# Convolution and gate of two batches on both query parts at once, with five head-pair slots and mask rows copied by engines

## The chip, the cores and the metric

The kernel runs on one core of one Trainium2 chip. A core has a matrix engine (TensorE, PE in the profile; its weight loads are listed as PEld), a vector engine (VectorE, DVE), a scalar engine (ScalarE, ACT), a general engine (GpSimd, POOL) and a queue engine that mostly issues transfers (SyncE, SP). The metric is the device time of one execution in microseconds. A profiled execution also has a span, which is the time from its first to its last instruction and lies a little below its device time.

## The reference, cut to what matters

Two layers follow each other. The first is block-sparse attention with 4 batches, 8 heads, 768 positions and 64 dimensions: blocks of 32 positions are seen if they are neighbours, first, last, or drawn at random. The second is a feed-forward layer with a gate that comes from a convolution along the sequence:

```python
scores = scale * np.matmul(q, k.transpose(0, 1, 3, 2))
scores = np.where(mask, scores, -1000000000.0)
attn = softmax(scores)                      # over the last axis
x = np.matmul(attn, v)                      # -> (4, 768, 512)
h = np.maximum(x @ w_in, 0.0)               # (4, 768, 1024)
hp = h with one zero position on each side
conv_out = sum(conv_w[k] * hp[:, k:k + S, :] for k in range(3))
gate = 1.0 / (1.0 + np.exp(-conv_out))
out = h * gate @ w_out                      # (4, 768, 512)
```

Inputs and output are float32; the matrix products run in bfloat16.

## The kernel before, in words

**Halves and units.** The 768 queries of a batch are cut into two parts of 384, so that there are 8 halves (`n`, with batch `b` and part `g`). The positions lie in tiles such that position p * 3 + c of a part is in column c * 128 + p, so neighbours along the sequence are 128 columns apart. Attention runs in 144 units, 18 to a half. A unit computes the transposed scores of eight 128x128 blocks on PE into `st` (L678), one exponential of 1024 columns on ACT into `pt` (L685), and the products with the values on PE into `av` (L705). The mask is added inside the score product: the operands have 88 rows, 64 of q or k and 24 that hold the mask in factored form.

**Head pairs and slots.** Heads are handled in 16 pairs, `P`. A pair's q and k come by DMA from POOL's queue (`swdge`, L492) as `nat`, and lie transposed in one of six slots: `ET` holds one head's part of each tile, `OT` the other. Pairs below `NPE` = 6 are transposed on PE (`pe_head`, L533) and moved from PSUM by four DVE copies (L539). Later pairs are transposed by two DMAs on SP's queue (L581) into `tmp`, then copied by two DVE copies of 1536 columns (L424). The 24 mask rows of slot 0 are computed at the start; slot 1 takes them by a DVE copy (ET) and a POOL copy (OT, L453), slots 2 to 5 by eight DMAs on SP's queue (L445).

**After attention.** `norm_ops` divides by the row sums on DVE (L629, L631), and the result is transposed to `xT`: by PE for half 0 and the last piece, else by DMAs on SP's queue (L652). `ffn1` multiplies with `w_in` on PE (L729) for each of eight 128-row chunks `ffc`, and a ReLU on ACT (L740) or DVE (L742), whichever the planner finds free, writes 384 columns into the middle of `hE` [128, 8, 640].

**Convolution and gate.** For two chunks at a time (4 times a half, 32 times in all) POOL copies shifted edges into `hE` (L829 to L835), so that each tap of the convolution is a shifted window of it. `conv_gate` then runs on DVE: three taps, each as two products of 384 columns with a per-partition weight (L753), two adds of 768 columns (L759). ACT applies tanh to 768 columns (L769), DVE adds 1 (L772) and multiplies with h into `gT` (L781). The last column of part 0 needs a neighbour in part 1: its partial sum is saved by POOL (`cvl`, L844), and completed after part 1's ReLUs by three small DVE instructions and a small tanh (L859, L860, L864, L867). `out_block` multiplies with `w_out` (L799), copies to `o2s` and stores through SP.

**What sets the order.** No engine order is written by hand. Each operation is given to `Scheduler` with the engines it may run on, a planned duration, its dependencies and the buffers that it takes and uses. `forward` builds the order of every engine: it takes repeatedly the operation that can start earliest, ties going to the higher priority; `backward` derives new priorities from the order found; `run` repeats this `PASSES` times. Buffers come from pools of fixed size (`P_he`, `P_cv`, `P_gt`, `P_slot` and so on) in turn. `FLEX` decides between ACT and DVE for the operations that either can do. Constants such as `OFF`, `F2A`, `XLAT`, `TLAT` and `S_FIRST` set the due times and assumed transfer latencies of the first pass.

Of the kernel before, what the change touches and what calls it, by code (L numbers as in the profile page):

```python
# [48 lines left out]
FLEX = 0.0345  # L49
# [4 lines left out]
class Scheduler:  # L54
# [108 lines left out]
    def backward(self, order):  # L163
# [34 lines left out]
        for o, t in zip(order, end):  # L198
            o.prio = -t
            o.outs = []  # L200
            for b in o.allocs:
                b.index = None
                b.pool.holders = []
# [10 lines left out]
def kernel(  # L214
# [21 lines left out]
    NSLOT = 6  # L236
    NPE = 6
# [21 lines left out]
    NTMP, NVN, NNAT, NPT, NXK, NXT, NHE, NCV, NGT, NOS = 2, 3, 3, 5, 3, 4, 3, 3, 4, 4  # L259
# [7 lines left out]
    hE_t = many(NHE, [128, NFFC, 640], BF16, "hE")  # L267
    m_t = many(NCV, [128, 2, 768], BF16, "m")
    tn_t = many(NCV, [128, 768], BF16, "tn")
    gT_t = many(NGT, [128, NFFC, 384], BF16, "gT")  # L270
# [48 lines left out]
    T0, PACE0, PACE1 = 8.0, 0.91, 1  # L319
    OFF = 32.0894  # L320
    XLAT, TLAT = 3.908, 9.2201
    S_FIRST, A_FIRST, R_FIRST, N_FIRST = 5.6663, -4, 0.1178, 0.842
    F1S, F2A, F2S = 0.03, 2.344, 0.191
    WO = 22.9467
    OFFL = 28
    PE_ = 0.0
    PASSES = 12
# [116 lines left out]
    def rows_to(dst, src):  # L444
        return lambda e: nc.sync.dma_start(out=dst[64:88], in_=src[64:88])  # L445

# [9 lines left out]
    for s in range(1, NSLOT):  # L456
        for t, m in ((ET, e_mask), (OT, o_mask)):
            if s == 1 and t is OT:
                m[s] = op({"POOL": 1.8}, pool_copy(t[s][64:88], t[0][64:88]), 2.5, [m[0]])
            elif s == 1:  # L460
                m[s] = op({"DVE": 0.58}, rows_by(t[s], t[0]), T(4.5 * s) - 2.5, [m[0]])
            else:
                m[s] = op({"SP": 0.46}, rows_to(t[s], t[0]), T(4.5 * s) - 6, [m[0]], lat=6.0,
                          earliest=T(18 + 2 * s) if s > 3 else 0.0)
# [4 lines left out]
    for s in range(NHE):  # L469
        def z(e, s=s):  # L470
            nc.vector.memset(hE_t[s][:, :, 639:640], 0.0)
        he_z[s] = op({"DVE": 0.15}, z, T(2))
# [24 lines left out]
    def qk_loads(P):  # L497
# [9 lines left out]
        k_iss[P] = ik  # L507
        return nb, lq, lk
# [41 lines left out]
    for P in range(NP):  # L550
# [23 lines left out]
        else:  # L574
# [12 lines left out]
            t0 = op({"SP": 1.3}, xp(0), due - 8, [lq], alloc=tb, uses=[nb], lat=TLAT)  # L587
            t1 = op({"SP": 1.3}, xp(1), due - 8, [lk], uses=[nb, tb], lat=TLAT)
            ce = op({"DVE": 0.5}, put(ET, 0), due, [t0, t1, slot_first.get(P - 1)], alloc=slot_b[P], uses=[tb])
            co = op({"DVE": 0.5}, put(OT, 64), due, [ce], uses=[slot_b[P], tb])  # L590
# [29 lines left out]
    def norm_ops(n, hp):  # L620
# [33 lines left out]
        xtr[(n, hp)] = op({"SP": 1.25}, tr, due - 5, [nm], lat=XLAT, uses=[xk] + us, alloc=al)  # L654
# [91 lines left out]
    def conv_gate(due, edge, relus, muls, gate_out, gate_h, heb, gtb, first_gt, last_tap=None):  # L746

        cb = Buf(P_cv)

        def mul(x, slot):  # L750
            def fn(e):
                for (o0, o1, src, w) in muls(x):
                    nc.vector.tensor_scalar(out=m_t[cb.index][:, slot, o0:o1], in0=src, scalar1=w, scalar2=None,  # L753
                                            op0=ALU.mult)
            return fn

        def add(e):
            m = m_t[cb.index]
            nc.vector.tensor_tensor(out=m[:, 0], in0=m[:, 0], in1=m[:, 1], op=ALU.add)  # L759
        nmul = len(edge[1])  # L760
        tm = sum(t_d4s(w_) for w_ in edge[1])
        m1 = op({"DVE": tm}, mul(1, 0), due + 1.7, list(relus) + [cw_op], alloc=cb, uses=[heb])
        m0 = op({"DVE": tm}, mul(0, 1), due + 2, [edge[0]], uses=[cb, heb])
        ad1 = op({"DVE": t_d2(768)}, add, due + 2.2, [m1, m0], uses=[cb])
        m2 = op({"DVE": tm}, mul(2, 1), due + 2.1, [edge[0], ad1], uses=[cb, heb])
        ad2 = op({"DVE": t_d2(768)}, add, due + 2.3, [ad1, m2], uses=[cb])
        if last_tap is not None:
            last_tap(cb, ad2, due)
        th = op({"ACT": 0.745}, lambda e: nc.scalar.activation(  # L769
            out=tn_t[cb.index], in_=m_t[cb.index][:, 0], func=AF.Tanh, bias=0.0, scale=0.5),  # L770
            due + 2.8 - R_FIRST, [ad2], uses=[cb])
        g1 = op({"DVE": t_d4(768)}, lambda e: nc.vector.tensor_scalar(  # L772
            out=tn_t[cb.index], in0=tn_t[cb.index], scalar1=1.0, scalar2=None, op0=ALU.add),
            due + 3.6, [th], uses=[cb])

        def gate(e):
            o, h = gate_out(), gate_h()
            t = tn_t[cb.index]
            if len(h.shape) == 3:
                t = t.rearrange("p (a b) -> p a b", a=2)  # L780
            nc.vector.tensor_tensor(out=o, in0=t, in1=h, op=ALU.mult)  # L781
        return op({"DVE": t_d2(768)}, gate, due + 3.7, [g1], uses=[cb, heb] + ([] if first_gt else [gtb]),
                  alloc=gtb if first_gt else None)

    def out_block(n, c, due, deps, parts=None):

        gb = gt_buf[n]
# [5 lines left out]
        for (mb, acc, take, o0, o1, on, by) in parts:  # L793
            ob = Buf(P_os)
            prev = None
            for a in range(4):
                def fn(e, a=a, acc=acc, o0=o0, o1=o1):
                    for ffc in (2 * a, 2 * a + 1):
                        nc.tensor.matmul(out=acc()[:, 0:o1 - o0], lhsT=gT_t[gb.index][:, ffc, 128 * c:128 * c + 128],  # L799
# [10 lines left out]
    heb_n, cvl_b, cvl_op, gates_n = {}, {}, {}, {}  # L810
    for n in range(NHALF):
        b, g = divmod(n, 2)
        lastn = n == NHALF - 1
        heb, gtb = Buf(P_he), Buf(P_gt)
        heb_n[n], gt_buf[n] = heb, gtb
        if g == 0:
            cvl_b[n] = Buf(P_cvl)
        relus, gates = [], []
        base = T(18 * (n + 1)) + (OFFL if lastn else OFF)
        for ffc in range(NFFC):  # L820
            due = base + W * F1S * ffc
            relus.append(ffn1(n, ffc, due, lambda ffc=ffc, heb=heb: hE_t[heb.index][:, ffc, 128:512], heb, ffc == 0))
            if ffc % 2 == 0:
                continue
            f0 = ffc - 1

            def edges(e, f0=f0, heb=heb, g=g, n=n):
                h = hE_t[heb.index]
                nc.gpsimd.tensor_copy(out=h[:, f0:f0 + 2, 1:128], in_=h[:, f0:f0 + 2, 384:511])  # L829
                nc.gpsimd.tensor_copy(out=h[:, f0:f0 + 2, 512:639], in_=h[:, f0:f0 + 2, 129:256])  # L830
                if g == 1:
                    nc.gpsimd.tensor_copy(out=h[:, f0:f0 + 2, 0:1],
                                          in_=hE_t[heb_n[n - 1].index][:, f0:f0 + 2, 511:512])
                else:
                    nc.gpsimd.memset(h[:, f0:f0 + 2, 0:1], 0.0)  # L835
            ed = op({"POOL": 1.0}, edges, due + 1.5, relus[f0:f0 + 2], uses=[heb] + ([heb_n[n - 1]] if g else []))

            def muls(x, f0=f0, heb=heb):
                return [(384 * y, 384 * y + 384, hE_t[heb.index][:, f0 + y, 128 * x:128 * x + 384],
                         cw[:, x, f0 + y:f0 + y + 1]) for y in range(2)]  # L840

            def save(cb, ad2, due, f0=f0, n=n):
                al = cvl_b[n] if f0 == 0 else None
                cvl_op.setdefault(n, []).append(op({"POOL": 0.2}, lambda e: nc.gpsimd.tensor_copy(  # L844
# [83 lines left out]
```

The softmax here doesn't subtract the row's maximum and nothing guards it: scores larger than these inputs give would overflow.

## Time and profile before

| | |
|---|---|
| Median of 13 runs | 215.76 us (214.45 to 219.64) |
| Profiled execution | 215.4 us, span 213.7 us |
| Granted TensorE clock | 1.0 throughout |
| Exponentials, L685 | 144, 1039 ns mean recorded duration |
| Products of the convolution, L753 | 192 of 128x384, 57.0 us busy |
| Adds of the convolution, L759 | 64 of 128x768, 35.1 us busy |
| Last exponential starts | about 182 us |
| Last gate (L781) starts | 206.62 us |

The page lists busy time, share of the span and instruction count of each engine. Recorded durations of DVE and ACT instructions that follow each other overlap, so the room that an instruction takes is read from the distance between two starts. A row of a table by stage gives the stretch in microseconds, its length, and for each engine the busy microseconds in it with the instructions in parentheses. The chain of work that ended last is followed back from the last instruction, each step to what released it or to the instruction before it on the same engine. In a row of the timeline stand the start, the duration, the engine, the line, the operation, the tiles written and read, and a count.

### The profile page before, as it was taken

Reading aid. Unit: us, or ns where it says so; the run is one execution under the profiler, and the core shown is the slowest. Engines: PE = TensorE matmul, PEld = TensorE weight load, DVE = VectorE, ACT = ScalarE, POOL = GpSimd, SP = SyncE. Lnnn points to the kernel's source line nnn. Section 1 sums busy time; section 2 is a strip of 40 time slices with the busy share of each in tenths; the row PEclk is TensorE's granted clock in tenths of the full one; section 3 lists DMA queues with packets and bytes.
Section 4 is the critical chain, followed back from the end, with each engine's and each line's share of the span. In section 5 each row is a group of like instructions: output and inputs, shape, how many; then the busy total and the mean of one; then the engine's idle time right before and its main releaser. Section 6 shows DMA issues by size and latency. Waiting matters only on the chain.

```text
span 213.7 us, 6605 instructions
## 1 busy us (share of the span) xinstructions
PE 199.3 (93%) x2596; PEld 150.1 (70%) x2596; DVE 190.3 (89%) x541; ACT 182.1 (85%) x227; POOL 80.0 (37%) x174
## 2 busy tenths in 40 slices
PE   7998999997999979999989999989999999998992
PEld 4787879885778857788767667767776787554441
DVE  6976539999999999399999999999999999999972
ACT  4597999999889989999989799889999999674541
POOL 8995206435524530355366202421241012443300
PEclk9999999999999999999999999999999999999999
DMA  6999997999999895999995993002100220122223
GB/s 164 146 197 208 199 202 111 122 161 159 168 147 212 114 122 67 167 190 191 153 132 102 128 194 107 18 21 67 52 23 21 85 102 21 27 90 101 100 98 147
DMA packets 50519, 25.84 MB, mean 121 GB/s; under 512 B 36320, under 2 KB 47352, under 8 KB 50488
## 3 DMA queue, kind: packets, MB, share of 16 engines
q0 software_dynamic: 18464, 11.14, 44.0%
q1 hardware_dynamic: 31592, 13.75, 31.2%
q10 hardware_dynamic: 432, 0.52, 0.8%
q8 instruction: 20, 0.33, 0.6%
q14 instruction: 11, 0.09, 0.2%
HBM read 23.08 MB, written 6.29 MB: 137 GB/s over the span
## 4 chain that ended last, share of the span: by engine, by line
DVE 56%; PE 25%; ACT 6%; issue 4%; DMA 4%; POOL 3%; ACTq 0%; POOLq 0%; DVEq 0%
DVE m L753 19%; DVE m L759 10%; PE st L678 8%; DVE hE L742 6%; DVE gT L781 5%; ACT pt L685 5%; DVE xtok L631 4%; PE mix L729 4%; PE av L705 4%; PE mix L799 4%; DMA nat<-in_k_dram 4%; DVE tn L772 3%; DVE o2s L424 2%; PE st L799 2%; PE av L371 2%
## 5 line engine op out<-in xcount | busy, mean ns | idle before, releaser
L685 ACT ACTIVATE pt<-st 128x1024 bf16<-128x1024 f32 x144 | 141.7, 1039 | 7.3 <-PE st L678 6.0
L705 PE MATMUL av<-vt,pt 128*128 128x65 bf16 x1152 | 57.9, 193 | 0.7 <-DVE xtok L631 0.3
L753 DVE TENSOR_SCALAR m<-hE,cw 128x384 bf16<-128x384 bf16 x192 | 57.0, 347 | 0.2
L705 PEld LDWEIGHTS <-pt 128*128 128x128 bf16 x1152 | 50.4, 97 | 5.0 <-ACT pt L685 0.7
L729 PE MATMUL mix<-xT,winb 128*128 128x384 bf16 x240 | 48.3, 325 | 2.3 <-DVE hE L742 1.1
L829 POOL COPY hE<-hE 128x254 bf16<-128x254 bf16 x32 | 17.2, 538 | 76.7 <-DVE hE L742 53.0
L799 PE MATMUL mix<-woutb,gT 128*128 128x512 bf16 x168 | 44.0, 379 | 1.9 <-DVE gT L781 1.5
L678 PE MATMUL st<-ot 88*128 88x128 bf16 (+1 forms) x224 | 42.5, 234 | 0.1
L678 PE MATMUL st<-et,ot 88*128 88x128 bf16 (+1 forms) x224 | 42.5, 234 | 0.0
L678 PE MATMUL st<-et 88*128 88x128 bf16 (+1 forms) x208 | 40.8, 239 | 1.7 <-ACT pt L685 1.7
L678 PEld LDWEIGHTS <-ot 88*128 88x128 bf16 x448 | 34.4, 97 | 10.2 <-issue 1.0
L678 PE MATMUL st<-ot,et 88*128 88x128 bf16 (+1 forms) x208 | 40.7, 239 | 0.5 <-ACT pt L685 0.2
L678 PEld LDWEIGHTS <-et 88*128 88x128 bf16 x416 | 32.2, 97 | 9.8 <-issue 3.1
L759 DVE TENSOR_TENSOR m<-m 128x768 bf16<-128x768 bf16 x64 | 35.1, 554 | 0.1
L769 ACT ACTIVATE tn<-m 128x768 bf16<-128x768 bf16 x32 | 27.7, 865 | 5.6 <-DVE m L759 5.5
L729 PEld LDWEIGHTS <-winb 128*128 128x128 bf16 x256 | 22.2, 97 | 13.2 <-issue 2.8
L799 PEld LDWEIGHTS <-gT 128*128 128x128 bf16 x200 | 16.5, 97 | 15.7 <-DVE gT L781 3.2
L742 DVE TENSOR_SCALAR hE<-mix 128x384 bf16<-128x384 f32 x37 | 20.2, 548 | 3.9 <-PE mix L729 3.8
L781 DVE TENSOR_TENSOR gT<-tn,hE 128x768 bf16<-128x768 bf16 x32 | 17.9, 563 | 0.1
L631 DVE TENSOR_TENSOR xtok<-av,rcp 128x384 bf16<-128x384 f32 x32 | 17.6, 549 | 0.3
L492 POOL DMA_DIRECT2D vn<-in_v_dram x16 | 11.4, 714 | 12.7 <-DVE vt L519 8.7
L740 ACT ACTIVATE hE<-mix 128x384 bf16<-128x384 f32 x23 | 11.9, 517 | 3.9 <-PE mix L729 3.3
(76 smaller groups left out, 172.2 us busy)
## 6 DMA issues: line engine op xcount, KB each, us to landing
out_dram<-o2s SPq DMA_DIRECT2D x23, 256.0 KB, 2.2
vn<-in_v_dram POOLq DMA_DIRECT2D x16, 192.0 KB, 6.0
nat<-in_q_dram POOLq DMA_DIRECT2D x15, 192.0 KB, 6.0
nat<-in_k_dram POOLq DMA_DIRECT2D x15, 192.0 KB, 6.7
winb<-in_moe_w_in_dram POOLq DMA_DIRECT2D x2, 512.0 KB, 10.7
woutb<-in_moe_w_out_dram POOLq DMA_DIRECT2D x2, 512.0 KB, 9.4
xT<-xtok SPq DMA_TRANSPOSE x27, 8.2
o2s<-in_k_dram ACTq DMA_DIRECT2D x2, 192.0 KB
```

The costliest lines, as they stand in the source:

```text
L631: nm = op({"DVE": 0.475}, lambda e: nc.vector.tensor_tensor(out=xtok_t[xk.index].rearrange("p c h d -> p h c d"), in0=o_of()[:, :, :, 0:64 ...
L678: nc.tensor.matmul(out=st_t[stb.index][:, 128 * x:128 * (x + n_)], lhsT=QK[kc % 2][s][0:88, 1, hh, kc // 2, :], rhs=QK[par][s][0:88, 0, hh ...
L685: e_op = op({"ACT": t_act(1024)}, lambda e, stb=stb, ptb=ptb: nc.scalar.activation(out=pt_t[ptb.index], in_=st_t[stb.index], func=AF.Exp, ...
L705: nc.tensor.matmul(out=av_t[av_buf[(n, P % 4)].index][:, off:off + 65], lhsT=pt_t[ptb.index][:, 128 * x:128 * x + 128], rhs=VT[P % NSLOT][ ...
L729: nc.tensor.matmul(out=tiles[hb.index][:, 0:384], lhsT=winb[:, fc, 128 * ffc:128 * ffc + 128], rhs=xT_t[xt_buf[n].index][:, fc, :], start= ...
L742: nc.vector.tensor_scalar(out=dst, in0=src, scalar1=0.5, scalar2=0.0, op0=ALU.mult, op1=ALU.max)
L753: nc.vector.tensor_scalar(out=m_t[cb.index][:, slot, o0:o1], in0=src, scalar1=w, scalar2=None, op0=ALU.mult)
L759: nc.vector.tensor_tensor(out=m[:, 0], in0=m[:, 0], in1=m[:, 1], op=ALU.add)
L769: th = op({"ACT": 0.745}, lambda e: nc.scalar.activation(out=tn_t[cb.index], in_=m_t[cb.index][:, 0], func=AF.Tanh, bias=0.0, scale=0.5), ...
L781: nc.vector.tensor_tensor(out=o, in0=t, in1=h, op=ALU.mult)
L799: nc.tensor.matmul(out=acc()[:, 0:o1 - o0], lhsT=gT_t[gb.index][:, ffc, 128 * c:128 * c + 128], rhs=woutb[:, ffc, o0:o1], start=(ffc == 0) ...
L829: nc.gpsimd.tensor_copy(out=h[:, f0:f0 + 2, 1:128], in_=h[:, f0:f0 + 2, 384:511])
```

## The change

- For batches 1 and 2 (`WIDE`), convolution and gate run once for both parts, two chunks at a time: 1536 columns in place of twice 768. `hE` and `gT` hold both parts of a batch, [128, 8, 2, 640] and [128, 8, 2, 384]. A product covers 2 x 384 columns; adds, tanh, "+1" and gate cover 1536. The edge copies on POOL cover both parts, with one copy for the column on each side of the seam, so the repair of the last column is left out for these batches. The tile `tn` is gone: tanh writes into the second half of `m`. Batches 0 and 3 remain at 768 columns.
- Pools: `NHE` 3 to 2, `NCV` 3 to 2, `NGT` 4 to 2, with tiles twice as wide.
- Slots: 6 to 5. `NPE` 6 to 4, so pairs 4 and 5 are transposed by DMA.
- Mask rows of slots 2 to 4 are copied by DVE; no DMA is used for them. The POOL copy for slot 1 follows the issue of pair 3's query load.
- The planner forgets the start and end times of a pass before the next, and `FLEX`, the due times, the assumed latencies and the number of passes have other values.
- `put_dma` is added, and is used for pairs from `PDMA` = 99 on, that is for none.

```diff
-FLEX = 0.0345
+FLEX = 0
...
             o.outs = []
+            o.start = o.end = None
...
-    NSLOT = 6
-    NPE = 6
+    NSLOT = 5
+    WIDE = (1, 2)
+    PDMA = 99
+    NPE = 4
...
-    NTMP, NVN, NNAT, NPT, NXK, NXT, NHE, NCV, NGT, NOS = 2, 3, 3, 5, 3, 4, 3, 3, 4, 4
+    NTMP, NVN, NNAT, NPT, NXK, NXT, NHE, NCV, NGT, NOS = 2, 3, 3, 5, 3, 4, 2, 2, 2, 4
...
-    hE_t = many(NHE, [128, NFFC, 640], BF16, "hE")
-    m_t = many(NCV, [128, 2, 768], BF16, "m")
-    tn_t = many(NCV, [128, 768], BF16, "tn")
-    gT_t = many(NGT, [128, NFFC, 384], BF16, "gT")
+    hE_t = many(NHE, [128, NFFC, 2, 640], BF16, "hE")
+    m_t = many(NCV, [128, 2, 1536], BF16, "m")
+    gT_t = many(NGT, [128, NFFC, 2, 384], BF16, "gT")
...
-    T0, PACE0, PACE1 = 8.0, 0.91, 1
-    OFF = 32.0894
-    XLAT, TLAT = 3.908, 9.2201
-    S_FIRST, A_FIRST, R_FIRST, N_FIRST = 5.6663, -4, 0.1178, 0.842
-    F1S, F2A, F2S = 0.03, 2.344, 0.191
-    WO = 22.9467
+    T0, PACE0, PACE1 = 8.0, 0.9137015439154899, 1.0
+    OFF = 23.744533411241996
+    XLAT, TLAT = 3.5, 4.920003434661278
+    PLAT = 4.0
+    XE = 2.0
+    S_FIRST, A_FIRST, R_FIRST, N_FIRST = 1.326, -0.8804424725948206, 0.08662063406836246, 0.41788067711119714
+    F1S, F2A, F2S = 0.03562311862501882, 1.3478278878287728, 0.27876112980595247
+    WO = 22.17656033584528
...
-    PASSES = 12
+    PASSES = 11
...
             if s == 1 and t is OT:
-                m[s] = op({"POOL": 1.8}, pool_copy(t[s][64:88], t[0][64:88]), 2.5, [m[0]])
-            elif s == 1:
+                m[s] = op({"POOL": 1.45}, pool_copy(t[s][64:88], t[0][64:88]), 2.5, [m[0]])
+            else:
                 m[s] = op({"DVE": 0.58}, rows_by(t[s], t[0]), T(4.5 * s) - 2.5, [m[0]])
-            else:
-                m[s] = op({"SP": 0.46}, rows_to(t[s], t[0]), T(4.5 * s) - 6, [m[0]], lat=6.0,
-                          earliest=T(18 + 2 * s) if s > 3 else 0.0)
...
+        if P == 3:
+            o_mask[1].deps.append(iq)
...
-    def conv_gate(due, edge, relus, muls, gate_out, gate_h, heb, gtb, first_gt, last_tap=None):
+    def conv_gate(due, edge, relus, hb, gb, f0, gs, first_gt, last_tap=None):
 
         cb = Buf(P_cv)
+        w = 768 * len(gs)
+        sl = slice(gs[0], gs[-1] + 1)
+
+        def m_of(slot):
+            return m_t[cb.index][:, slot, 0:w]
+
+        def split(ap):
+            return ap.rearrange("p (y g s) -> p y g s", y=2, g=len(gs))
 
         def mul(x, slot):
             def fn(e):
-                for (o0, o1, src, w) in muls(x):
-                    nc.vector.tensor_scalar(out=m_t[cb.index][:, slot, o0:o1], in0=src, scalar1=w, scalar2=None,
-                                            op0=ALU.mult)
+                for y in range(2):
+                    nc.vector.tensor_scalar(
+                        out=split(m_of(slot))[:, y], in0=hE_t[hb.index][:, f0 + y, sl, 128 * x:128 * x + 384],
+                        scalar1=cw[:, x, f0 + y:f0 + y + 1], scalar2=None, op0=ALU.mult)
             return fn
...
-            if ffc % 2 == 0:
+            if ffc % 2 == 0 or wide and g == 0:
                 continue
             f0 = ffc - 1
...
+            both = wide or g == 1
+            gs = [0, 1] if wide else [g]
+
+            def edges(e, f0=f0, heb=heb, g=g, gs=gs):
+                h = hE_t[heb.index][:, f0:f0 + 2]
+                for (d0, d1, s0) in ((1, 128, 384), (512, 639, 129)):
+                    if len(gs) == 2:
+                        nc.gpsimd.tensor_copy(out=h[:, :, :, d0:d1], in_=h[:, :, :, s0:s0 + 127])
+                    else:
+                        nc.gpsimd.tensor_copy(out=h[:, :, g, d0:d1], in_=h[:, :, g, s0:s0 + 127])
                 if g == 1:
-                    nc.gpsimd.tensor_copy(out=h[:, f0:f0 + 2, 0:1],
-                                          in_=hE_t[heb_n[n - 1].index][:, f0:f0 + 2, 511:512])
-                else:
-                    nc.gpsimd.memset(h[:, f0:f0 + 2, 0:1], 0.0)
...
+                    nc.gpsimd.tensor_copy(out=h[:, :, 1, 0:1], in_=h[:, :, 0, 511:512])
+                if len(gs) == 2:
+                    nc.gpsimd.tensor_copy(out=h[:, :, 0, 639:640], in_=h[:, :, 1, 128:129])
+                elif g == 0 and heb is not he_buf[0]:
+                    nc.gpsimd.memset(h[:, :, 0, 639:640], 0.0)
+            srcs = relus[f0:f0 + 2] + (relu_n[n - 1][f0:f0 + 2] if both else [])
...
-        if g == 1:
+        dp = base + W * (F1S * 8 + 0.04)
+        if g == 1 and not wide:
...
+            if wide:
+                todo = [(m, c, gates_n[n]) for m in (n - 1, n) for c in range(3)] if g else []
+            else:
+                todo = [(n, c, gates_n[n]) for c in range(2 + g)] + ([(n - 1, 2, [[p3o]] * 4)] if g else [])
```

## The prediction

> **What bounds the kernel now.** I read the page's busy shares and chain first, then the waits from 103 us on, then busy time by stage, then VectorE (DVE) instruction by instruction. The busy shares of the page:
>
> ```profile
> span 213.7 us, 6605 instructions
> PE 199.3 (93%) x2596; PEld 150.1 (70%) x2596; DVE 190.3 (89%) x541; ACT 182.1 (85%) x227; POOL 80.0 (37%) x174
> ```
>
> Three engines are near full, so the chain has to say whose work sets the end:
>
> ```profile
> DVE 56%; PE 25%; ACT 6%; issue 4%; DMA 4%; POOL 3%; ACTq 0%; POOLq 0%; DVEq 0%
> DVE m L753 19%; DVE m L759 10%; PE st L678 8%; DVE hE L742 6%; DVE gT L781 5%; ACT pt L685 5%; DVE xtok L631 4%; PE mix L729 4%; PE av L705 4%; PE mix L799 4%; DMA nat<-in_k_dram 4%; DVE tn L772 3%; DVE o2s L424 2%; PE st L799 2%; PE av L371 2%
> ```
>
> The convolution and gate on DVE (L753 products, L759 adds, L772, L781) make 37% of the chain. By stage (columns: stretch, its length, then busy us and instructions of PE, PEld, DVE, ACT, POOL; the rest is clock and DMA):
>
> ```profile
> 0.00:19.00 19.00, 16.09 (x198) 12.82 (x199) 14.36 (x48) 12.98 (x17) 15.64 (x27) 1.00 1.06 175
> 19.00:44.00 25.00, 24.40 (x412) 21.46 (x411) 17.90 (x44) 23.39 (x25) 9.43 (x18) 1.00 1.20 166
> 44.00:82.00 38.00, 34.95 (x508) 27.44 (x505) 37.09 (x105) 35.58 (x43) 15.71 (x33) 1.00 1.18 149
> 82.00:103.00 21.00, 21.00 (x306) 16.90 (x305) 16.56 (x45) 20.25 (x25) 8.52 (x19) 1.00 1.28 162
> 103.00:133.00 30.00, 28.70 (x387) 21.59 (x385) 29.77 (x86) 27.54 (x34) 11.33 (x26) 1.00 0.90 137
> 133.00:183.00 50.00, 48.46 (x660) 37.12 (x657) 49.62 (x145) 48.00 (x61) 11.88 (x35) 1.00 0.16 46
> 183.00:205.50 22.50, 21.32 (x124) 10.51 (x122) 22.31 (x68) 13.01 (x24) 7.53 (x18) 1.00 0.21 83
> ```
>
> From 103 us to the last gate at 206.6 DVE is 99% busy, and the list of waits for 103 to 206.5 us names none of DVE. PE is second with 1.3 + 1.5 + 1.2 = 4.0 us idle by its records. From 82 to 103 PE is full and DVE idles 4.4; from 19 to 44 ACT and PE set the pace.
>
> The slots of the DVE instructions are read as distances between starts, since the recorded durations overlap:
>
> ```profile
> 141.23 0.56 DVE L759 TENSOR_TENSOR m<-m 128x768 bf16<-128x768 bf16 x1
> 141.71 0.55 DVE L631 TENSOR_TENSOR xtok<-av,rcp 128x384 bf16<-128x384 f32 x1
> 142.18 0.35 DVE L772 TENSOR_SCALAR tn<-tn 128x768 bf16<-128x768 bf16 x1
> 142.44 0.54 DVE L753 TENSOR_SCALAR m<-hE,cw 128x384 bf16<-128x384 bf16 x2
> 142.90 0.55 DVE L781 TENSOR_TENSOR gT<-tn,hE 128x768 bf16<-128x768 bf16 x1
> 143.37 0.55 DVE L759 TENSOR_TENSOR m<-m 128x768 bf16<-128x768 bf16 x1
> 143.84 0.54 DVE L424 COPY et<-tmp 64x1536 bf16<-64x1536 bf16 x1
> 144.31 1.45 DVE L753 TENSOR_SCALAR m<-hE,cw 128x384 bf16<-128x384 bf16 x6
> 145.68 1.01 DVE L759 TENSOR_TENSOR m<-m 128x768 bf16<-128x768 bf16 x2
> ```
>
> A product takes 0.23 us (two in 0.46, six in 1.37), an add or gate 0.47, the "+1" 0.27, a one-source copy of 1536 columns 0.47.
>
> **The change part by part.** The sum is made against the profiled execution, 215.4 us (span 213.7 and 1.7 around it); the median shown is 215.76, 0.36 higher.
>
> *Wide convolution, batches 1 and 2.* Two narrow tiles cost 12 products, 4 adds, 2 "+1", 2 gates: 2.76 + 1.88 + 0.54 + 0.94 = 6.12 us. For the wide tile: 768 more columns of a one-source bf16 operation cost 0.47 - 0.27 = 0.20, so a product of 768 costs 0.23 + 0.10 = 0.33 and a "+1" of 1536 costs 0.47. For two sources, 8 columns (L860) take 0.08 and 768 take 0.47, so 1536 take 0.87. Six products, two adds, "+1" and gate: 1.98 + 1.74 + 0.47 + 0.87 = 5.06. Eight wide tiles in place of sixteen narrow ones: 8 x 1.06 = 8.5 us less on DVE, all of it behind 89 us, where the third half's ReLUs begin. Bounds: if the two-segment source ran at half the rate, a wide product would cost two narrow ones and only 8.5 - 48 x 0.13 = 2.3 us would go. The copy into vt at L519 argues against it: strided, 768 columns, and it takes 0.27 like the contiguous L772. At the other end, products average 57.0/192 = 0.30 where GpSimd runs beside them; if that extra 0.07 goes per instruction, 48 x 0.07 = 3.4 us more go. I take 8.5.
>
> "VectorE: DVE Perf Modes" of the Trainium skill (the errata section) puts the fixed part at about 150 cycles, 0.156 us, paid once per instruction. By it the 80 removed instructions would be worth 12.5 us, as an estimate. The rows give 0.07 to 0.13 because the next instruction starts inside that time.
>
> *The seam column.* Wide tiles need no repair: two times L859, L860, L867 (0.19 + 0.08 + 0.08) go, 0.7 us of DVE, with 8 copies to cvl on POOL. POOL's edge copies become 508 columns instead of 254 (two for four). POOL is a third busy, its waits are for ReLUs; cost nothing while DVE has other tiles, else some 0.4 us per wide tile, 3 in all, inside the wait priced below. Eight tanh fewer save ACT their fixed part: the tanh takes a slot of 0.74 for 768 columns and the exponential 0.90 for 1024, slope 0.16 per 256, so 0.74 - 3 x 0.16 = 0.26 at most each, 2 us of an engine that is not last here.
>
> *Waiting for both parts.* A wide tile needs ReLUs of both halves. Batch 1 costs nothing: the old gates of half 2 run from 106 to 120 us, and half 3's last exponential is at 88.5, so that with 8.2 us for xT its ReLUs can be had from 98. Batch 2 does cost. From 100 to 140 us DVE executed 42 products, seven narrow tiles or 21.4 us, so other work (norms, copies, ReLUs, slowed products) took 46%. Batch 1's 20.2 us then last from 103 to 103 + 20.2/0.54 = 140. Half 5's last exponential is at 136; 8.2 us for the transposition of its last xtok and two ReLUs bring the first wide tile of batch 2 to about 148. Of those 8 us other work covers 46%: DVE idles W = 4 us, queued behind the first wide product being only the tiles that follow. Bounds 0 (the planner runs attention ahead) and 12 (half 5 is as late as in the old order, whose ReLUs of it start at 149 and end at 159.5).
>
> *Pairs 4 and 5 by DMA transposition.* Gone: 24 PE transpositions (0.056 each, 1.3 us) and 8 PSUM copies (slots of 0.54 from 35 to 43 us, 4.3 us). New: 4 copies of 1536 columns (2.0 us) and 4 DMA transpositions of 1.2 to 2.5 us on SP's queue, 6.5 us to land. So 2.3 us less DVE work. Their inputs are requested at 14.6 to 20.0 us, attention on them begins at exponential 37, 46 us: over 15 us of cover. They stand before xT's transpositions on SP, the first of which is at 34.4. Without cover, each transposition in line delays the next by 1.5 to 2.5 us, 6 to 8 together.
>
> *Mask rows.* Eight DMAs of 72 KB leave SP (six between 7.5 and 12.1 us); six copies of 24x1536 come to DVE, 0.47 by the 64-row copy to 0.87 by the one at 9.15 us, which ran beside POOL's: 2.8 to 5.2 us. DVE has gaps of 8.2 us between 12.9 and 31 us and hides all but those of slots 2 and 3, which come into a run without gaps up to 12.9 us: +1 us taken, bounds 0 and +2. What the DMAs leave free, 0.44 MB at 200 GB/s, 2.2 us, may let pair 3's keys land sooner (PE waits 1.0 us at 17.8): worth 0 to 1, taken as 0. The POOL copy for slot 1 is moved behind the issue of pair 3's query load, ending 1.5 us later, 11.1 us; pair 1 is used at 12: nothing, or 1 us.
>
> "GPSIMD Engine Reference" of the Trainium skill (Specifications) says that GpSimd's SBUF interfaces contend with DVE instructions that use two ports or two SBUF inputs. That speaks against mask rows on DVE beside POOL; the 0.87 agrees, and by it all six copies would be at the upper bound, 5.2 us.
>
> *Five slots, fewer and larger buffers, planner.* Each slot is free 18 units before its next use, and two convolution tiles are enough while one tile's products (2.3 us) exceed tanh and hand-over (about 1.5): nothing. ReLUs shift between ACT and DVE with FLEX 0, and the planner now forgets old times before it counts a buffer free: between -2 and +2, taken as 0.
>
> *Sum.* From 103 us: -8.5 - 0.7 + 4 = -5.2, cut to PE's idle of 4.0: -4.0. Before: -2.3 of DVE from 35 to 82 us, of which I count 1.0, because 82 to 103 is PE's and gains only its 1.3; masks +1.0. Total -4.0: 211.4 for the profiled execution, 211.8 as a median.
>
> **Rivals.** *Wait for both parts (slower).* Place: DVE between the tiles of batches 1 and 2. The last stage's saving of 9.2 is used up at W = 9.2, with half 5's first ReLUs past 158. With W = 12: 215.76 + 2.8 = 218.6. For: DVE is already without work from 85 to 89 us. Against: relieved DVE frees buffers sooner.
> *PE takes over.* If half of PE's 4 us cannot be filled, the gain is 4 - 2 = 2: 213.8. For: PE full from 82 to 103.
> *All of it arrives.* W near 0 and the masks hidden: PE's 4.0, 2.0 before 82 us, and 1.5 of the 7.1 us behind the last gate: 208.3. Against: that PE must not idle.
> *Pairs 4 and 5 late.* PE and ACT stall near 46 us by up to 8, partly caught up: 215.76 - 4 + 8 = 219.8 at worst. Against: the 15 us of cover.
> *Narrow pace.* Products at half rate save 2.3 instead of 8.5, and W = 4 eats it: 3.0 - 4 = +1.0 and nothing elsewhere, 216.8.
>
> **How the numbers follow.** A difference under 0.3%, 0.65 us, cannot be told from none here. Forecast (210 to 213.5) 0.40; PE takes over 0.17, of it 0.03 within the limit; all of it 0.13; wait for both 0.18, of it 0.03 within; pairs late 0.06; narrow pace 0.06, of it 0.02 within. Faster 0.40 + 0.14 + 0.13 = 0.67; within 0.08; slower 0.15 + 0.06 + 0.04 = 0.25. Leaving out a tenth at each end gives 207.5 to 218.
>
> **What would show it.** Right: 96 narrow and 48 wide products, the wide with slots near 0.33; adds near 0.87; DVE below 184 us busy; a DVE gap of about 4 us between 135 and 150; PE closer to full behind it. Wrong: wide products near 0.46; gaps of DVE over 9 us behind 103; PE waiting for tmp-fed copies near 46 us; an attention end (old: 183 us) that comes no earlier while the tail behind it is over 30 us.

## The result, and the profile after

The changed kernel takes 218.63 us as a median (216.91 to 220.62), the kernel before 215.24 in the runs beside it: a ratio of 1.0144 with a 95% interval from 1.0112 to 1.0176. The change makes the kernel slower, by 1.4%; the forecast was 211.8. The first two lines of the profile after, and its chain of waits:

```profile
span 216.8 us, 6457 instructions
PE 199.5 (92%) x2572; PEld 148.9 (69%) x2572; DVE 183.1 (84%) x457; ACT 183.9 (85%) x218; POOL 81.0 (37%) x146
DVE 53%; PE 16%; issue 14%; DMA 7%; ACT 5%; POOL 1%; DVEq 0%; ACTq 0%; POOLq 0%; SPq 0%
DVE m L771 17%; DVE m L777 10%; DMA tmp<-nat 7%; DVE gT L790 6%; PE st L688 5%; ACT pt L695 5%; DVE hE L752 4%; DVE m L788 4%; PE mix L739 3%; DVE xtok L641 3%; PE av L715 3%; DVE et L428 3%; PE mix L809 2%; DVE ot L428 2%; PE av L375 2%
```

DVE lost 190.3 - 183.1 = 7.2 us of work, and the span grew by 3.1, so DVE's idle time grew from 23.4 to 33.7 us. On the chain there is a new item, the DMA transposition of a head pair into `tmp`, with 7% of the span. "Issue", 4% before, has 14%; most of it is one piece of 11.75 us from 97.8 us on, at the end of which POOL copies the edges of the first wide tile, and POOL's list of waits names a ReLU on DVE there. PE is as busy as before (199.3 then), with 24 instructions fewer. The same stages as before the change (stretch, length, then busy us and instructions of PE, PEld, DVE, ACT, POOL):

```profile
0.00:19.00 19.00, 15.53 (x193) 12.38 (x194) 17.02 (x52) 11.91 (x15) 17.05 (x29) 1.00 1.07 162
19.00:44.00 25.00, 24.49 (x404) 20.91 (x401) 18.47 (x49) 24.66 (x29) 9.10 (x16) 1.00 1.36 176
44.00:82.00 38.00, 34.72 (x502) 27.29 (x499) 34.60 (x96) 36.28 (x43) 15.89 (x29) 1.00 1.07 153
82.00:103.00 21.00, 20.41 (x296) 16.25 (x295) 11.06 (x28) 19.78 (x24) 6.17 (x8) 1.00 1.36 163
103.00:133.00 30.00, 27.31 (x367) 21.11 (x367) 27.94 (x58) 26.14 (x30) 12.04 (x21) 1.00 0.66 104
133.00:183.00 50.00, 48.74 (x655) 36.71 (x654) 46.67 (x98) 47.70 (x55) 12.67 (x26) 1.00 0.26 58
183.00:205.50 22.50, 21.85 (x143) 11.13 (x140) 22.43 (x72) 14.14 (x25) 8.08 (x18) 1.00 0.25 88
```

DVE now idles 9.9 us between 82 and 103 (4.4 before), 2.1 between 103 and 133 (0.2 before) and 3.3 between 133 and 183 (0.4 before). PE's idle time grew where it matters: from 0 to 0.6 us in the fourth stage and from 1.3 to 2.7 in the fifth. What DVE waited for over the whole execution (in total, times, longest, in us), and the instructions around the longest wait:

```profile
DVE et L428 <- DMA tmp<-nat: 9.2, 4, 5.3
DVE hE L752 <- PE mix L739: 7.3, 8, 3.0
```
```profile
95.44 0.56 DVE L752 TENSOR_SCALAR hE<-mix 128x384 bf16<-128x384 f32 x1 [1.47 <-PE mix L739]
101.28 0.55 DVE L428 COPY et<-tmp 64x1536 bf16<-64x1536 bf16 x1 [5.28 <-DMA tmp<-nat]
...
109.36 1.09 DVE L771 TENSOR_SCALAR m<-hE,cw 128x768 bf16<-128x768 bf16 x2
```

The list of waits of before has no wait for `tmp`. Now four of its transpositions are late, at 67 to 69, 89 to 90, 96 to 101 and 105 to 107 us; these belong to later pairs (8, 10, 11 and 12), not to pairs 4 and 5. Their transpositions took 5.8, 7.1, 10.7 and 6.9 us to land. The first wide product starts at 109.4, while before the products of half 2 started at 91.7.

The new instructions cost what was forecast. Starts in a quiet stretch of batch 2:

```profile
163.11 0.94 DVE L790 TENSOR_TENSOR gT<-m,hE 128x1536 bf16<-128x1536 bf16 x1
163.98 0.18 DVE L639 RECIPROCAL rcp<-av 128x6 f32<-128x6 f32 x1
164.09 1.36 DVE L771 TENSOR_SCALAR m<-hE,cw 128x768 bf16<-128x768 bf16 x4
165.37 0.54 DVE L641 TENSOR_TENSOR xtok<-av,rcp 128x384 bf16<-128x384 f32 x1
...
168.21 0.55 DVE L788 TENSOR_SCALAR m<-m 128x1536 bf16<-128x1536 bf16 x1
168.68 0.95 DVE L777 TENSOR_TENSOR m<-m 128x1536 bf16<-128x1536 bf16 x1
```

Four wide products take (165.37 - 164.09) = 1.28 us, 0.32 each (0.33 forecast); the gate 163.98 - 163.11 = 0.87 (0.87), the "+1" 0.47 (0.47).

### The profile page after: what moved, and what is told of

Read it like the earlier page. It is cut to its first block, busy times and chain, and to the rows that moved or that the text cites. A ratio compares the mean times of both kernels' runs of the same rounds, so it can differ in the third digit from the quotient of the medians.

```text
span 216.8 us, 6457 instructions
## 1 busy us (share of the span) xinstructions
PE 199.5 (92%) x2572; PEld 148.9 (69%) x2572; DVE 183.1 (84%) x457; ACT 183.9 (85%) x218; POOL 81.0 (37%) x146
## 4 chain that ended last, share of the span: by engine, by line
DVE 53%; PE 16%; issue 14%; DMA 7%; ACT 5%; POOL 1%; DVEq 0%; ACTq 0%; POOLq 0%; SPq 0%
DVE m L771 17%; DVE m L777 10%; DMA tmp<-nat 7%; DVE gT L790 6%; PE st L688 5%; ACT pt L695 5%; DVE hE L752 4%; DVE m L788 4%; PE mix L739 3%; DVE xtok L641 3%; PE av L715 3%; DVE et L428 3%; PE mix L809 2%; DVE ot L428 2%; PE av L375 2%
## 5 line engine op out<-in xcount | busy, mean ns | idle before, releaser
L771 DVE TENSOR_SCALAR m<-hE,cw 128x384 bf16<-128x384 bf16 (+1 forms) x144 | 49.4, 393 | 1.0 <-POOL hE L849 0.6
L777 DVE TENSOR_TENSOR m<-m 128x768 bf16<-128x768 bf16 (+1 forms) x48 | 33.1, 696 | 0.1
L847 POOL COPY hE<-hE 128x254 bf16<-128x254 bf16 x32 | 18.0, 591 | 40.5 <-DVE hE L752 29.6
L739 PEld LDWEIGHTS <-winb 128*128 128x128 bf16 x256 | 22.5, 97 | 14.4 <-issue 3.3
L786 ACT ACTIVATE m<-m 128x768 bf16<-128x768 bf16 (+1 forms) x24 | 25.5, 1064 | 7.0 <-DVE m L777 6.9
L845 POOL COPY hE<-hE 128x508 bf16<-128x508 bf16 x16 | 11.2, 728 | 50.5 <-DVE hE L752 43.0
L752 DVE TENSOR_SCALAR hE<-mix 128x384 bf16<-128x384 f32 x38 | 20.8, 548 | 7.3 <-PE mix L739 7.3
L790 DVE TENSOR_TENSOR gT<-m,hE 128x768 bf16<-128x768 bf16 (+1 forms) x24 | 16.6, 690 | 0.0
L493 POOL DMA_DIRECT2D nat<-in_q_dram x15 | 12.2, 811 | 6.0 <-issue 4.0
```

The source lines that it names most:

```text
L739: nc.tensor.matmul(out=tiles[hb.index][:, 0:384], lhsT=winb[:, fc, 128 * ffc:128 * ffc + 128], rhs=xT_t[xt_buf[n].index][:, fc, :], start= ...
L752: nc.vector.tensor_scalar(out=dst, in0=src, scalar1=0.5, scalar2=0.0, op0=ALU.mult, op1=ALU.max)
L771: nc.vector.tensor_scalar(out=split(m_of(slot))[:, y], in0=hE_t[hb.index][:, f0 + y, sl, 128 * x:128 * x + 384], scalar1=cw[:, x, f0 + y:f ...
L777: nc.vector.tensor_tensor(out=m_of(0), in0=m_of(0), in1=m_of(1), op=ALU.add)
L786: th = op({"ACT": t_act(w) + 0.055}, lambda e: nc.scalar.activation(out=m_of(1), in_=m_of(0), func=AF.Tanh, bias=0.0, scale=0.5), due + 2. ...
L790: return op({"DVE": t_d2(w)}, lambda e: nc.vector.tensor_tensor(out=gT_t[gb.index][:, f0:f0 + 2, sl], in0=split(m_of(1)), in1=hE_t[hb.inde ...
```

## The experiments

Three explanations were to be told apart: the wide tiles' waits for the second part use up DVE's saving; the late `tmp` transpositions use it up; PE sets the pace, and what DVE saves has little room. The letters in an expectation are its own and mean what it says of them.

**Is DVE's work still worth anything?** First, the order of the changed kernel, with each wide DVE instruction issued as two narrow ones:

```diff
-                    nc.vector.tensor_scalar(out=split(m_of(slot))[:, y], in0=hE_t[hb.index][:, f0 + y, sl, ...
+                    for i, g in enumerate(gs):
+                        nc.vector.tensor_scalar(out=split(m_of(slot))[:, y, i], in0=hE_t[hb.index][:, f0 + y, g, ...
```

> The order of every engine is that of the changed kernel; only each wide DVE instruction of convolution and gate is issued as two narrow ones (products of 384 columns, adds, +1 and gates of 768), the tanh stays wide. That puts back the 8.5 us of DVE work that the wide tiles save, 4.2 behind 109 us and 4.2 behind 150 us. Theory A (DVE sets the pace as soon as wide tiles may start, the saving is real but is lost in front of them, where DVE waits for the ReLUs of both parts): 5 to 8 us over the changed kernel, 224 to 227 us. Rival (PE has taken over, DVE has room behind 109 us): at most 2 us over it, 219 to 220.5 us.

Measured: 228.30 us, ratio 1.0639 (1.0576 to 1.0703). DVE was busy 193.0 us, 9.9 more than in the changed kernel, and the ratio is 0.0495 above the changed kernel's, 10.7 us. Work added to DVE behind the waits is paid in full. (PE's granted clock is 0.50 for 6.8 us from 182 us on in this run, but DVE is busy all through that stretch, so it is DVE that sets the pace there.) The other direction, from the kernel before and later from a repaired version of the changed one (`e3_early`, next section): the second add of each tile of batches 1 and 2 is left out, 7.5 and 7.0 us of DVE.

```diff
+        skip = heb in [heb_n.get(x) for x in (2, 3, 4, 5)]
-        ad2 = op({"DVE": t_d2(768)}, add, ...
+        ad2 = op({"DVE": t_d2(768)}, (lambda e: None) if skip else add, ...
```

> The kernel before, in its own order, with the second add left out in the 16 tiles of batches 1 and 2 (the third tap is missing from their convolution): 16 x 0.47 = 7.5 us less DVE work in the same places as the wide tiles save it, but with no tile waiting for a second part. Theory A (DVE sets the pace there, up to PE's 4 us): 4 us less than before, 210 to 211.5 us. Rival (PE has taken over already, no DVE saving of any form helps): less than 1.5 us, 213.3 us or more.

> The run with early transpositions with the second add left out in the eight wide tiles (third tap missing from batches 1 and 2): 8 x 0.87 = 7.0 us less DVE work behind 109 us. If DVE sets the pace behind the wait there too: 4 to 6 us less than that run, 209.5 to 211.5 us. If the wait for both parts and PE set it: at most 2 us less, 213.4 us or more.

Measured: 212.14 us, ratio 0.9853 (0.9779 to 0.9928), and 211.43, ratio 0.9828 (0.9803 to 0.9853) against 1.0025 of its base. So 7 us less DVE work, with no wait added, is worth 3.1 to 4.2 us, not 7; the forecast had put the limit at PE's 4.0. The first of the two figures is loose: its four runs lie between 210.78 and 214.30. The stages 103 to 133 and 133 to 183 of the second one show where the rest goes:

```profile
103.00:133.00 30.00, 30.00 (x422) 23.61 (x420) 29.53 (x63) 29.37 (x34) 10.59 (x20) 1.00 0.59 90
133.00:183.00 50.00, 49.86 (x646) 36.76 (x643) 44.34 (x103) 47.20 (x56) 12.49 (x30) 1.00 0.20 58
```

PE is full there: 79.86 of 80 us. In these stages nothing more can be had from DVE.

**The late transpositions.** A fourth `nat` buffer alone, the order unchanged:

```diff
-    nat_t = many(NNAT, ...
+    nat_t = many(4, ...
+        for i, b in enumerate(P_nat.holders):
+            b.index = i % 4
```

> Same order on every engine as the changed kernel, but the loads of q and k go round four nat buffers instead of three, so POOL no longer waits 3.8 us for the transposition of an earlier pair before it can request a load, and the transpositions into tmp can start up to 4 us sooner. Theory B (late tmp transpositions, for which DVE waits 9.2 us in four places, make the loss): 1.5 to 3 us less than the changed kernel, 215.5 to 217 us, with DVE's wait for tmp under 5 us. Theory A (the wait of wide tiles for both parts makes it): within 0.7 us of the changed kernel, 218 to 219.3 us.

Measured: 220.41, ratio 1.0278 (1.0240 to 1.0315), which neither figure covers. The wait for `tmp` stayed (8.9 us in all, 6.7 the longest), so the buffer alone was not what was short. In this run PE stands still from 103 to 105 us behind the longest wait, and its granted clock is then 0.50 for 3.4 us; in the changed kernel the clock stays at 1.00 there. This fits with it being slower still, but wasn't tried alone. Next, four `nat` and three `tmp` buffers, and the loads and transpositions of pairs 6 to 15 up to 4 us earlier in the order of POOL and SP; DVE, ACT and PE keep the order of the changed kernel:

```diff
+        sizes, before_, moved = {P_nat: 4, P_tmp: 3}, {}, set()
...
+                if pool is P_nat and i >= 6:
+                    moved.update(u for u in b.users if u.eng in ("POOL", "DQ", "SP"))
+        for o in sorted(moved, key=lambda o: (o.start, o.key)):
+            after = list(o.deps) + [u for b in o.allocs for u in before_[b]]
+            key[o] = min(key[o], max([o.start - EARLY] + [key[u] + 0.001 for u in after]))
```

> As the one with four nat buffers, with three tmp buffers too, and the loads of pairs 6 to 15 and their transpositions up to 4 us (of planned time) earlier in the queues of POOL and SP; DVE, ACT and PE keep the order of the changed kernel. DVE's wait for tmp should all but go (from 9.2 to under 2 us). Theory B: 2 to 3.5 us less than the changed kernel, 215 to 216.6 us, so no more than 0.6% over the kernel before. Theory A: within 1 us of it, 217.6 to 219.5 us, since DVE then waits for ReLUs in the same place.

Measured: 215.42, ratio 1.0025 (1.0000 to 1.0050). No DVE wait for `tmp` is left. The late transpositions cost 1.0144 - 1.0025 = 1.2%, 2.6 us (1.7 to 3.4 by the two intervals), most of the loss. Single transpositions still take up to 11.0 us to land; they are issued early enough. The third `tmp` buffer and the earlier place were not tried apart. But with DVE at 183.7 us, 6.6 less than before, the kernel is only level with the kernel before. Its stages from 82 us on:

```profile
82.00:103.00 21.00, 20.84 (x304) 16.75 (x303) 12.52 (x31) 19.80 (x23) 6.13 (x8) 1.00 1.51 165
103.00:133.00 30.00, 29.25 (x402) 22.87 (x401) 29.69 (x62) 28.74 (x33) 11.35 (x20) 1.00 0.58 98
133.00:183.00 50.00, 48.75 (x648) 36.21 (x647) 46.67 (x100) 47.27 (x54) 13.63 (x29) 1.00 0.18 51
```

DVE idles 8.5 us in the first of them and 3.3 in the third. PE idles 0.16 + 0.75 + 1.25 = 2.2, against 0 + 1.3 + 1.5 = 2.8 before.

**The wait for both parts, by itself.** Here the wide tiles of a batch read part 0 alone, in the same shapes, so the wait is gone while the work stays. The base is `e3_early`. First with the order kept, and then with the tiles of batch 1 up to 8 us earlier in it:

```diff
-in0=hE_t[hb.index][:, f0 + y, sl, 128 * x:128 * x + 384],
+in0=(hE_t[hb.index][:, f0:f0 + 2, 0, 128 * x:128 * x + 384] if part0 else ...
...
+                key[o] = min(key[o], max([o.start - AHEAD] + [key[p] + p.end - p.start + 0.16 for p in after]))
```

> Control for the next kernel. The order of the kernel with early loads (215.42 us, ratio 1.0025) on every engine, but the four wide tiles of batch 1 read part 0 in place of both parts (products: the chunk pair of part 0; gate: four chunks of part 0; edge copies of part 0 twice), so that they need no ReLU of half 3; same instruction shapes and counts. The output of batch 1 is therefore not the reference's. Both theories: 215 to 216, since the instructions stand in the order where they stood, behind the work that filled the wait (ratio 1.000 to 1.005).

> The control with one thing more: since the tiles of batch 1 need part 0 alone, their instructions stand up to 8 us earlier in the order of DVE, POOL and ACT (first wide product planned at 95.1 in place of 103.1), everything else in its order. The work is the same, so what changes is the wait for both parts in batch 1. Theory A (the wait of batch 1, taken as nothing in the forecast, costs about 4 us of DVE idle time between 82 and 103 us): DVE idle there falls from 8.5 to some 4, and the time falls by 2 to 4 us, to 211.5 to 213.5, ratio 0.981 to 0.994. Rival (DVE idles there because PE sets the pace between 82 and 103, and the lost time is elsewhere): within 1 us of the control, 214.5 to 216.

Measured: 218.18, ratio 1.0125 (1.0078 to 1.0171), and 216.86, ratio 1.0062 (1.0031 to 1.0092). The control missed: it should have stayed at 215.4. Its list of DVE's waits from 103 to 133 us begins:

```profile
DVE et L430 <- DMA tmp<-nat: 4.3, 1, 4.3
```

POOL's edge copies no longer waited 14.1 us for half 3's ReLUs, so the loads behind them in POOL's queue went out at 93 to 98 us instead of 107 to 112.5. Transpositions between 88 and 116 us then took 10.1 us to land as a median, in the base 5.7. So the second pair of kernels leaves POOL alone: the three taps read the middle window of part 0, the edge copies stay and wait as they did.

```diff
-0, 128 * x:128 * x + 384] if part0
+0, 128:512] if part0
```

> Control for the next two. The order of the kernel with early loads (215.42 us, ratio 1.0025) on every engine. The wide tiles of batch 1 read the middle 384 columns of part 0 for all three taps, and four chunks of part 0 for the gate, so they need neither a ReLU of half 3 nor the edge copies; POOL's edge copies stay as they were, wait for half 3 as before, and nobody uses them in this batch. Shapes and counts are unchanged; the convolution of batch 1 is therefore not computed. In the earlier control POOL no longer waited 14.1 us for half 3, issued three loads of the heads' inputs some 13 us earlier, and a tmp transposition came 4.3 us late. If that is why it took 218.2, this one is back at 215 to 216 (ratio 1.000 to 1.006); if reading part 0 is itself slow, it stays at 218.

> The control with the DVE and ACT instructions of batch 1's wide tiles up to 8 us earlier in the order (first wide product planned at 95.1 in place of 103.1). Theory A (the wait of batch 1 by itself costs the time): DVE idle between 82 and 103 us falls by some 4 us and so does the time, 211.5 to 213.5. Theory B (DVE only runs into the next wait, that for half 5, earlier): the idle time moves to the stage from 133 to 183 us, and the time falls by less than 1.5 us, 214 to 216.

> As the kernel before it, and the wide tiles of batch 2 too read part 0 (half 4) alone and stand up to 8 us earlier (first wide product planned at 135.1 in place of 143.1): the convolutions of batches 1 and 2 are not computed. Both waits for the second part are gone, the work is the same. Theories A and B: 211 to 213 (ratio 0.980 to 0.991), as the kernel with 7 us less DVE work behind the waits (211.43). Rival C (PE sets the pace, the waits for both parts cost nothing): 214.5 to 216, within 1 us of the control.

Measured: 215.35, ratio 1.0005 (0.9979 to 1.0032): the control holds, so it was POOL's queue. But 217.68, ratio 1.0116 (1.0086 to 1.0146), and 218.04, ratio 1.0143 (1.0117 to 1.0169), with the waits gone: against both theories and the rival. The middle one from 103 us on:

```profile
103.00:133.00 30.00, 26.61 (x364) 20.66 (x362) 29.80 (x58) 27.37 (x30) 12.40 (x20) 1.00 0.64 87
133.00:183.00 50.00, 48.97 (x661) 37.10 (x658) 41.85 (x92) 46.82 (x54) 12.70 (x26) 1.00 0.19 51
```

PE lost 29.25 - 26.61 = 2.6 us between 103 and 133, and DVE then idled 8.2 us behind 133. PE's waits in that stretch, which in the control are 0.7 us for ReLUs on DVE and nothing else:

```profile
PE av L717 <- DVE xtok L643: 1.3, 1, 1.3
PE st L690 <- ACT pt L697: 0.9, 1, 0.9
PE mix L741 <- ACT hE L752: 0.5, 1, 0.5
PE mix L741 <- DVE hE L754: 0.5, 1, 0.5
```

This fits moved tiles that push back other work of DVE: the division that frees `av` for PE, and half 3's ReLUs (POOL's longest wait for them is 16.2 us in place of 14.1). Convolution that is done sooner gains nothing when it delays what PE waits for. So only the first tile of a batch was moved, into the place where DVE idled:

```diff
-        for n0, cb, relus, chain in ahead:
+        for n0, cb, relus, chain in ahead[0::4]:
```

> As the control e11_same (215.35 us; batch 1's wide tiles read the middle of part 0 alone, so batch 1's convolution is not computed), and of batch 1's four tiles only the first stands up to 8 us earlier on DVE and ACT (first product planned at 95.1), where DVE idled 8.5 us between 82 and 103 us; the other three keep their places and move up only as DVE gets to them. So the wait is filled, and the ReLUs of half 3 are not pushed back as they were when all four tiles were moved (217.68). Theory A (the wait of batch 1 costs time): PE idle from 103 to 133 stays below 1 us and the time falls by 1 to 3 us, 212.3 to 214.3. Rival (behind 82 us PE is already full, 50.1 of 51 us up to 133, so DVE's idle time there costs nothing): 214.6 to 216.

> As the kernel before it, for batches 1 and 2 (both convolutions are not computed): the first tile of batch 2 too stands up to 8 us earlier (planned at 135.1), where DVE idled 3.3 us between 133 and 183. Theory A: 1 us less than the kernel before it or more, 211 to 213.3. Rival (PE full, 48.75 of 50 us in that stage): at most 1 us less than the control, 214.3 to 216.

Measured: 214.50, ratio 0.9974 (0.9956 to 0.9992), and 214.17, ratio 0.9970 (0.9953 to 0.9986). The first one's stages from 82 us on:

```profile
82.00:103.00 21.00, 20.88 (x304) 16.72 (x303) 15.44 (x37) 19.70 (x24) 5.97 (x8) 1.00 1.28 173
103.00:133.00 30.00, 29.05 (x404) 22.88 (x402) 27.36 (x56) 28.85 (x32) 10.91 (x20) 1.00 0.61 92
133.00:183.00 50.00, 48.91 (x648) 36.42 (x646) 46.67 (x100) 46.95 (x55) 13.64 (x30) 1.00 0.18 51
```

DVE does 2.9 us more in the fourth stage and then idles 2.6 in the fifth: the idle time has moved, and PE's columns hardly change. By the ratios, filling the place ahead of batch 1 is worth 1.0005 - 0.9974 = 0.3%, 0.7 us, and that ahead of batch 2 another 0.1 us. The intervals of the control and of the first kernel overlap, so the gain is hardly clear of none: both together 0.0035, 0.75 us (0.1 to 1.4 by the two intervals). The first kernel lies between the figures of theory A and of the rival, the second just under the rival's. So DVE's idle time in these places costs little while PE is near full. The other three tiles of each batch kept their places, so this is what filling two places gives, and not the whole price of waiting for both parts.

**Narrow tiles with the rest of the change.** These ask what slots, pairs, masks and due times do without the wide tiles. Other tiles need other due times, so each kernel has its own set:

```diff
-    WIDE = (1, 2)
+    WIDE = ()
...
-    OFF = 23.744533411241996
+    OFF = 27.424617724312814
...
```

> The changed kernel with narrow tiles in all batches (five slots, masks by engines, pairs 4 and 5 by DMA kept), due times and number of passes searched anew for it, with transpositions early as in the run of that name, so that neither is a handicap. 7 to 8 us more DVE work than the run with early transpositions, but no tile waits for a second part. Theory A (the wait for both parts costs what wide tiles save): 213 to 216 us, level with the run with early transpositions. Rival (wide tiles are worth their saving, and slots, masks and pairs 4 and 5 have eaten it): 219 us or more.

> Narrow tiles in all batches with the rest of the change, no early transpositions, but the planner assumes 6.0 us for a transposition of xtok and 7.5 us for one into tmp (the change assumed 3.5 and 4.9, 2 more at the start; the changed kernel's trace has medians of 3.7 and 6.0, up to 11), due times searched anew. Theory B (late transpositions because of short assumed latencies): DVE waits under 2 us for tmp, and with narrow tiles 213 to 215.5 us. Rival (the assumed latencies do not matter): DVE waits for tmp as in the changed kernel, 217 us or more.

> As the narrow run with early transpositions, but from due times with which ACT begins with the first cast of pair 0, as in the changed kernel, so that the first exponential is at 8 us again and not at 9.9. Theory A: without that false start narrow tiles are level with wide ones, 214.5 to 216.3 us, with 6 to 8 us more DVE work and as much less DVE idle time. Rival (wide tiles are worth most of their saving): still 217 us or more.

Measured: 217.35, ratio 1.0102 (1.0065 to 1.0138); 216.60, ratio 1.0051 (1.0021 to 1.0082); 219.23, ratio 1.0172 (1.0139 to 1.0205). None is as fast as the kernel before; the first two lie between the figures of their theory and their rival, the third has the rival's. They spread over 2.6 us with the due times, so the price of narrow against wide can't be read from them. The last has one stall: a `tmp` transposition issued at 46.7 us landed 13.3 us later, and the granted clock of PE was 0.50 for 6.8 us behind it (last section). The same was tried with one wide batch (`WIDE = (1,)` and `(2,)`):

> Wide tiles in batch 1 alone (narrow in 0, 2 and 3), early transpositions, due times searched anew. Half the saving, 4.6 us of DVE work, against one wait. Theory A: DVE idles 8 us or more between 82 and 110 us in front of batch 1's tiles and under 1.5 us from 133 to 183; 214.5 to 216.5 us. Rival (each wide batch is worth its saving of 2 to 4 us over narrow tiles): 2 us under the narrow run.

> Wide tiles in batch 2 alone, early transpositions, due times searched anew. Half the saving against the other wait. Theory A: DVE idles 4 to 5 us from 82 to 103 as in the kernel before, and about 3 us between 133 and 160 in front of batch 2's tiles; 214 to 216 us. Rival (each wide batch is worth its saving): 2 us under the narrow run.

Measured: 231.67, ratio 1.0734 (1.0665 to 1.0803), and 218.36, ratio 1.0105 (1.0038 to 1.0172). Neither expectation holds. Both stall for `tmp` (11.2 and 2.1 us of DVE's time), the first near 50 to 75 and 110 to 123 us for `xT` as well; as times they tell of transpositions, not of the wait for both parts. In the second, DVE idles 6.2 of the 27 us from 133 to 160, while PE is busy for 26.8 of them: again idle time of DVE in front of a wide tile with PE full.

## Why the prediction was wrong

- *Wide convolution, the seam column, pairs 4 and 5 on DVE.* Right in kind. Products, "+1", adds and gates have the forecast slots, and DVE is 7.2 us less busy (below 184, as said). Over 19 to 82 us DVE lost 54.99 - 53.07 = 1.9 us, where the forecast took off 2.3 for the pairs; convolution work moved in these stages too, so this is no separate test of that term.
- *Mask rows and start.* Not tried alone, but nothing here goes beyond the forecast's 0 to 2. The ninth exponential is 1.7 us late (18.1 against 16.4), but the 45th is level (56.9 against 57.1).
- *Planner, "between -2 and +2, taken as 0".* This step failed: 2.6 us through late transpositions. The diff showed the assumed latency of a `tmp` transposition cut from 9.22 to 4.92 us (6.92 below pair 8), and the traces show landings up to 10.7 us after the change and 7.0 at most before. The forecast looked at pairs 4 and 5, which were not late, and at no later pair. That the shorter assumption is what put them late wasn't tried alone (`e7_narrow_lat` assumes 7.5 us, but with narrow tiles and due times of its own); that an earlier place in the order, with a third `tmp` buffer, takes the wait away is shown by `e3_early`.
- *"Batch 1 costs nothing" and W = 4 for batch 2.* Without the late transpositions, DVE's idle time between 82 and 103 us is still 8.5 - 4.4 = 4.1 us above that of before (the narrow tiles of half 2 no longer fill that place, and the wide ones need half 3). Ahead of batch 2 it is 3.3 - 0.4 = 2.9 us, near the forecast W. But the price is not the idle time: filled with one tile each, the two places gave 0.7 and 0.1 us. The 88.5 us that the forecast gives for half 3's last exponential is the one before it; the last starts at 89.85, which changes little. The rival "wait for both parts" names 218.6, the measured value, by W = 12 in batch 2, which is not what happened: that the figures agree is chance.
- *The cut "to PE's idle of 4.0: -4.0".* As a limit of what DVE's saving can give it held roughly: 7.5 and 7.0 us less of DVE gave 3.1 and 4.2. That the change would get there is the second step that failed, and the larger one: without the late transpositions 1.0025 was measured where the forecast is 211.8 / 215.76 = 0.9816, 4.5 us apart. PE idled 4.0 us from 82 to 205.5 before and 0.2 + 0.75 + 1.25 + 0.65 (21.84 of 22.5) = 2.8 in `e3_early`: 6.6 us of saving on DVE took 1.2 from PE's idle time, and the time stayed level with before. The further 7.0 in `e6_after_less` brought PE to 79.86 of 80. The rival "PE takes over" expected such idle time of PE to stay, and gave it 2 us.
- *The signs.* One of those named for being wrong came: the last exponential starts at 184.5 us (182.4 before), with 32 us behind it.

In sum: of the saving of 7.2 us on DVE, about 4 could count beside PE; the late transpositions took 2.6, and the two filled places gave back about 0.75. What stays open is about 2.5 us (0.9 to 4.2 by the two intervals): with the loads early and the two places filled the change stands at 0.997, and the kernel before with 7.5 us of DVE left out at 0.985. The profiles of these two, `e13_first12` and `e5_before_less`, have 14.1 and 11.2 us of idle time on PE; 0.9 us of the difference lies before 82 us. The narrow kernels suggest that the open part comes from the other parts of the change and its due times, but don't separate these, and `e4_narrow` has 4.1 us more DVE work than the kernel before.

## What to carry to other kernels

Before counting a saving on one engine, read the second-busiest engine in the same stages: its idle time is roughly the ceiling (here 2.8 and 4.0 us of PE, where 7.0 and 7.5 us less on DVE gave 4.2 and 3.1), and a change may reach little of it. When a tile is made larger, list what used to fill the time in which it now waits, and for every constant that places transfers, compare the assumed latency with the landings in the trace, for all users and not only the changed ones. An instruction that waits in a queue that also issues loads sets when those loads start, and freeing it can hurt.

## What the runs showed of the hardware

A stall of PE can cost more than its length. In `e8_narrow_start` PE had little to do from 50 us on, and the granted clock (the column after POOL) fell to half:

```profile
50.00:56.00 6.00, 1.90 (x30) 1.27 (x26) 3.35 (x10) 2.85 (x3) 0.00 (x0) 0.94 1.42 133
56.00:62.00 6.00, 4.92 (x37) 3.45 (x38) 3.56 (x10) 2.66 (x3) 2.43 (x4) 0.50 1.39 185
62.00:66.00 4.00, 3.96 (x64) 3.30 (x63) 2.73 (x8) 3.69 (x5) 1.42 (x2) 0.98 1.87 134
```

At half the clock the six microseconds from 56 on gave 37 matrix products, the four behind them 64. A product of 128x512 took 628 ns as a mean between 58 and 62 us, and 379 behind it. "TensorE: Matmul & The Clock Gate" of the Trainium skill (Part 1, the clock gate) says that an idle window of about 3.4 us halves the clock, and a busy one of that length restores it. The lengths fit here: the half clock lasted 6.8 us in this run, from 55.3 on, with PE full from 58 on, 3.4 us in `e2_nat4` (from 106.5) and `e10_part0_same` (from 109.8), and 6.8 in `e1_split` (from 182.1). But no gap of PE ahead of these stretches is as long as 3.4 us: they are 1.9 and 2.3 us with a little work between them in this run, and 2.4, 2.5 and 1.9 us in the other three. A stretch in which PE was only in part idle was enough.

The landing time of a DMA transposition between two on-chip tiles isn't a constant: a median of 5.7 us in one stretch of the order, 10.1 in the same stretch with three loads sent some 14 us earlier, and up to 15.8 us in `e8_narrow_start`.
